# Groups of dummy matmuls in many tile shapes behind the last output matmul

## The chip, the cores and the metric

The kernel runs on one core of a Trainium2 chip. The metric is the device time of one execution in microseconds (us), the median over the runs.

## The reference

What is computed is attention with 32 global tokens and a local window, followed by a feed-forward block, over 8 batches with 8 heads of 64:

```python
s_g = scale * np.matmul(q_g, k_all.transpose(0, 1, 3, 2))      # 32 global queries see all 544 keys
out_g = np.matmul(sm(s_g), v_all)
mask = np.abs(pos[:, None] - pos[None, :]) <= 32               # 512 local queries see a window
s_ll = np.where(mask, scale * np.matmul(q_l, k_l.transpose(0, 1, 3, 2)), -1000000000.0)
s_lg = scale * np.matmul(q_l, k_g.transpose(0, 1, 3, 2))       # and the 32 global keys
out_l = np.matmul(sm(np.concatenate([s_lg, s_ll], axis=-1)), np.concatenate([v_g, v_l], axis=2))
x = np.concatenate([out_g, out_l], axis=2)...                  # (8 * 544, 512)
h = x @ w_in                                                   # 512 -> 2048
out = (h * (1.0 / (1.0 + np.exp(-1.702 * h)))) @ w_out         # 2048 -> 512, float32
```

## The kernel before

Operands are bfloat16 and sums are in float32 in PSUM. The program works in quads: one quad is four heads of one batch, so there are 16 quads, two to a batch. The order of the instructions on each engine is the order in which the code is written (`tc.manual_schedule()`); pools of tiles add the waits where a buffer is used again.

For a quad, `S` (L314) multiplies keys with queries. The contraction is over 32 partitions at a time (64 numbers per head lie as 32 float32 words of two bfloat16 each, and `e` picks one of the two). Four heads sit in four groups of 32 partitions, so four matmuls with tiles of 32 rows and 128 columns go to four PSUM banks. The queries are read in a window: `q[p, lo:hi, r0 : r0 + nr, e]` takes runs of 10 or 12 elements at a stride of two, 200 or 228 in all. `gk` (L333) uses tiles of 32 rows and 32 columns for the global keys, either 32 or 512 columns of queries wide. `ekU` (L400) and `U` (L426) multiply the exponentials with values; `U` has tiles of 128 rows and 32 columns, four heads side by side in one bank. `Gm` (L444) does the global queries with the same tiles and 66 columns. ScalarE takes the exponentials (L347), VectorE the mask product `M` (L354, bfloat16, both operands in SBUF), the transposes and the normalisation (`R`, `XL`, `G`).

The feed-forward block of batch i has `h_mm` (L495, full 128x128 tiles, 512 columns of tokens), `h_act` (tanh on ScalarE, L502, and a product on VectorE into `gT`, L503) and `o_mm` (L520, 512 columns). The attention quads of the next batch are placed between the `o_mm` groups. The global tokens of all batches form a ninth, narrow block (256 tokens). The last steps are

```python
    for st in range(4):
        o_mm(B, st)
    o_out(B, 1, None)
```

where `o_out` with its last tile runs the 16 accumulating matmuls twice (L532), for columns 0 to 320 and 320 to 512. ScalarE copies each part out of PSUM (L534), and SyncE and ScalarE issue the DMAs to the output (L542).

Names that the change uses: `warm` is a tile of zeros, [128, 512] in bfloat16, that `keep` (L165) and `zero` (L555) already read for dummy matmuls. `qtiles[0]` is the tile of transposed queries, [128, 24, 32] in float32, that `S` reads as bfloat16 pairs. `psP` is a pool of four PSUM banks (tag "p"); `psS` has two tiles of two banks each (tags "s0" and "s1"); `bank(pt, i)` is bank i of that pair of tiles. `att` is a pool of SBUF tiles with two buffers for each name (`rs`, `sT`, `e0`, `e1`). `mask` holds the window masks, and LW and RW are 352 and 428. The pieces of code that place a matmul's tile are the partition slices of its operands: the rows follow from the partitions of `lhsT`, the columns from the partitions of the output.

Of the kernel before, what the change touches and what calls it, by code (L numbers as in the profile page):

```python
# [12 lines left out]
F32 = mybir.dt.float32  # L13
BF16 = mybir.dt.bfloat16
# [783 lines left out]
    o_out(B, 1, None)  # L798


# [1 line left out]
_INS = ['q_l', 'k_l', 'v_l', 'q_g', 'k_g', 'v_g', 'moe_w_in', 'moe_w_out']  # L802
_OUTS = [((4352, 512), 'float32')]
# [25 lines left out]
```

## Time and profile before

The median of two runs is 307.42 us (307.30 and 307.54). The page has one profiled execution:

| | |
|---|---|
| span of the profiled execution | 305.3 us |
| median of the runs less the span | 2.1 us |
| TensorE matmuls | 298.7 us busy (98%), 3265 of them |
| TensorE weight loads | 148.5 us (49%), 3265 |
| VectorE / ScalarE / GpSimd | 211.2 / 169.3 / 55.7 us busy |
| granted TensorE clock | full in all 40 slices |
| o_mm (L520) | 122.0 us, 528 matmuls |
| h_mm (L495) | 108.9 us, 496 matmuls of 512 columns |
| S (L314) | 21.2 us, 528 matmuls |

The profiled execution's own time beyond its span is not on the page; the span runs from its first instruction to its last, and what the metric counts around it is taken as the 2.1 us between the span and the median. In the page a matmul's duration includes its way through the array, so matmuls that run one behind the other overlap; how often they start is read from their starts in the timeline. "PE" is the row of the matmuls and "PEld" that of the weight loads.

### The profile page before, as it was taken

To read this page: it belongs to the slowest core of one execution; us is meant where nothing else is said; L and a number is where in the kernel's file an instruction comes from. 1 tells how busy PE (TensorE), PEld (TensorE's weight loads), DVE (VectorE), ACT (ScalarE), POOL (GpSimd) and SP (SyncE) were. 2 spreads that over 40 slices of the span, in tenths; PEclk is the share of its full clock that TensorE was granted. 3 is DMA by queue.
4 is the path that set the end of the run, shared out by engine and by line. 5 is a ranking of instruction groups with operands and counts; after the bars stand their busy time and mean duration, and the time that the engine had idled before them with its cause. 6 is when DMAs were issued, how large, how long until landed. Compare 5 with 4: busy or idle time off the path is not lost.

```text
span 305.3 us, 7862 instructions
## 1 busy us (share of the span) xinstructions
PE 298.7 (98%) x3265; PEld 148.5 (49%) x3265; DVE 211.2 (69%) x445; ACT 169.3 (55%) x282; POOL 55.7 (18%) x89
## 2 busy tenths in 40 slices
PE   7999999999999999999999999999999999999995
PEld 6454445445454455445454455445454454446653
DVE  6678858978868876777767876787677855573320
ACT  4738484585556655575457654665456661673421
POOL 8732755530050002300050002100000000000000
PEclk9999999999999999999999999999999999999999
DMA  7999999999399023941299024901130021101122
GB/s 191 178 206 207 197 180 230 211 170 131 82 112 191 10 56 84 151 97 37 54 122 170 4 56 89 101 0 48 44 86 2 2 66 48 46 0 36 36 63 75
DMA packets 56436, 29.52 MB, mean 97 GB/s; under 512 B 43088, under 2 KB 46288, under 8 KB 56400
## 3 DMA queue, kind: packets, MB, share of 16 engines
q0 software_dynamic: 46000, 16.98, 49.9%
q1 hardware_dynamic: 9920, 11.39, 14.3%
q10 hardware_dynamic: 480, 0.66, 0.7%
q8 instruction: 25, 0.41, 0.6%
q14 instruction: 11, 0.09, 0.1%
HBM read 35.13 MB, written 8.91 MB: 144 GB/s over the span
## 4 chain that ended last, share of the span: by engine, by line
PE 80%; DMA 15%; DVE 2%; POOL 1%; issue 1%; ACT 0%; ACTq 0%; DVEq 0%; POOLq 0%
PE op L520 34%; PE hp L495 33%; DMA rk<-in_k_l_dram 10%; PE s L314 5%; PE ov L426 4%; DMA rq<-in_q_l_dram 3%; DMA w_in_sb<-in_moe_w_in_dram 2%; PE ov L400 2%; DVE xL L459 1%; PE op L532 1%; PE s L444 1%; PE s L333 1%; ACTq L542 0%; ACT ob L534 0%; DVE e L354 0%
## 5 line engine op out<-in xcount | busy, mean ns | idle before, releaser
L520 PE MATMUL op<-w_out_sb,gT 128*128 128x512 bf16 x528 | 122.0, 380 | 0.0
L503 DVE SCALAR_TENSOR_TENSOR gT<-th,hp 128x512 bf16<-128x512 f32 (+1 forms) x140 | 91.2, 657 | 41.8 <-ACT th L502 40.7
L495 PE MATMUL hp<-xL,w_in_sb 128*128 128x512 bf16 x496 | 108.9, 379 | 0.3 <-DVE xL L459 0.2
L502 ACT ACTIVATE th<-hp 128x512 f32<-128x512 f32 (+1 forms) x140 | 79.9, 573 | 43.4 <-PE hp L495 39.9
L495 PEld LDWEIGHTS <-w_in_sb 128*128 128x128 bf16 x576 | 56.2, 98 | 64.7 <-issue 0.9
L520 PEld LDWEIGHTS <-gT 128*128 128x128 bf16 x528 | 49.2, 98 | 56.2 <-issue 3.5
L347 ACT ACTIVATE e<-s 128x856 bf16<-128x856 f32 x62 | 51.6, 884 | 12.1 <-PE s L444 7.0
L534 ACT ACTIVATE ob<-op 128x512 f32<-128x512 f32 (+2 forms) x35 | 20.5, 585 | 59.0 <-PE op L520 56.5
L89 POOL DMA_DIRECT2D v<-in_v_l_dram x24 | 18.7, 782 | 111.2 <-PE s L444 105.8
L450 DVE STREAM_TRANSPOSE sT<-ov 128x512 f32<-128x512 f32 x15 | 10.8, 717 | 26.9 <-PE ov L426 26.9
L354 DVE TENSOR_TENSOR e<-e,mask 128x1408 bf16<-128x1408 bf16 x28 | 24.4, 872 | 5.7 <-ACT e L347 5.7
L314 PE MATMUL s<-q,kT 32*128 32x228 bf16 (+5 forms) x528 | 21.2, 280 | 1.0 <-DVE q L275 1.0
L459 DVE TENSOR_TENSOR xL<-ov,rs 128x512 bf16<-128x512 f32 x30 | 19.3, 686 | 1.4
L314 PEld LDWEIGHTS <-kT 32*128 32x128 bf16 x528 | 10.9, 95 | 14.8 <-issue 6.6
L271 DVE STREAM_TRANSPOSE kT<-rk 128x512 f32<-128x512 f32 (+1 forms) x17 | 16.9, 994 | 1.0 <-DMA rk<-in_k_l_dram 1.0
L383 ACT ACTIVATE ek<-kb 128x512 bf16<-128x512 f32 x16 | 9.7, 608 | 9.2 <-PE kb L333 7.0
L426 PE MATMUL ov<-e,v 128*32 128x160 bf16 (+1 forms) x480 | 12.2, 239 | 0.0
L454 DVE STREAM_TRANSPOSE rs<-rT 128x512 f32<-128x512 f32 x16 | 11.4, 711 | 0.6
L275 DVE STREAM_TRANSPOSE q<-rq 128x512 f32<-128x512 f32 (+1 forms) x17 | 10.9, 641 | 1.0 <-ACT rq L558 1.0
L426 PEld LDWEIGHTS <-v 128*32 128x32 bf16 x512 | 10.0, 97 | 0.9 <-issue 0.9
L333 PE MATMUL kb<-q,kgT 32*32 32x512 bf16 x128 | 10.4, 387 | 0.0
L495 PE MATMUL hp<-xG,w_in_sb 128*128 128x256 bf16 x64 | 9.6, 273 | 0.0
(82 smaller groups left out, 170.6 us busy)
## 6 DMA issues: line engine op xcount, KB each, us to landing
out_dram<-ob SPq DMA_DIRECT2D x132, 64.0 KB, 1.7
v<-in_v_l_dram POOLq DMA_DIRECT2D x32, 128.0 KB, 6.0
rk<-in_k_l_dram POOLq DMA_DIRECT2D x6, 512.0 KB, 10.8
rq<-in_q_l_dram POOLq DMA_DIRECT2D x5, 512.0 KB, 8.6
w_out_sb<-in_moe_w_out_dram POOLq DMA_DIRECT2D x4, 512.0 KB, 10.8
rq<-in_q_l_dram POOLq DMA_DIRECT2D x5, 256.0 KB, 8.9
ek<-ek SPq DMA_DIRECT2D x13, 96.0 KB, 2.9
w_in_sb<-in_moe_w_in_dram POOLq DMA_DIRECT2D x4, 256.0 KB, 6.4
```

Of the source, the lines that this page charges most:

```text
L89: nc.gpsimd.dma_start(out=vtiles[b % 2][p, s, :, :, :D], in_=vf[b, g][:, hs])
L271: nc.vector.transpose(self.kT.rearrange("p (r t) -> p t r", t=16)[:, lo:hi], loaded[self.b][0][:, self.u].bitcast(F32)[:, 32 * lo : 32 * hi])
L314: nc.tensor.matmul(ps[j][:, off : off + n], lhsT=self.k[p, 128 * c : 128 * c + 128, e], rhs=self.q[p, lo:hi, r0 : r0 + nr, e], start=(e == ...
L347: nc.scalar.activation(e[:, 2 * i : 2 * i + 2, :RW], self.ps[i][:, :, :RW], AF.Exp, scale=scale)
L354: nc.vector.tensor_mul(e, e, mask[:, rnd : rnd + 1, :].to_broadcast([128, 4, LW]))
L426: nc.tensor.matmul(ov[32 * j : 32 * j + 32, :].rearrange("p (t r) -> p t r", t=16)[:, :, r0 : r0 + nr], lhsT=lv, rhs=self.E[c // 2][:, j, ...
L459: nc.vector.tensor_mul(self.x[:, 2 * self.u + h, :], self.st[1 + h], self.st["rs"])
L495: nc.tensor.matmul(hp[:, : width(i)], lhsT=w_in_c[:, fc // 8, kc, fc % 8 // 2, :, fc % 2], rhs=(xL[i] if i < B else xG)[:, kc, :], start=( ...
L502: nc.scalar.activation(th[:, :n], hp[:, :n], AF.Tanh, scale=0.851)
L503: nc.vector.scalar_tensor_tensor(gTs[i][:, fc, :n], in0=th[:, :n], scalar=1.0, in1=hp[:, :n], op0=ALU.add, op1=ALU.mult)
L520: nc.tensor.matmul(op, lhsT=gTs[i][:, fc, tci * 128 : tci * 128 + 128], rhs=w_out_sb[:, fc, :], start=(first and fc == 4 * f4), stop=(fc = ...
L534: nc.scalar.activation(ob[:, lo:hi], op[:, lo:hi], AF.Copy, scale=0.5)
```

## The change

Behind `o_out(B, 1, None)` the program gets further work whose results nothing reads. `plain` issues full matmuls of 512 columns into one bank of `psP`. `tiles` issues, for every repetition, one matmul for each tile of the given rows and columns, row groups outside and column groups inside; row group i writes bank i, column group g writes its partitions. Between them the moving operand is straight (`near0`), a window of the queries (`runs`), or evenly strided (`flat`). At the end VectorE gets two fills and a reciprocal, a fill and a mask product, and GpSimd a fill, a mask product and a copy.

```diff
     o_out(B, 1, None)
 
 
+    keys = qtiles[0].bitcast(BF16).rearrange("p t (r e) -> p t r e", e=2)
+    flat = keys.rearrange("p t r e -> p (t r) e")
+
+    def tiles(name, rows, cols, n, reps, rhs, w=None):
+        pt = [psS.tile([128, 2, 512], F32, name=name, tag="s%d" % i) for i in range(2)]
+        for k in range(reps):
+            for i in range(128 // rows):
+                for g in range(128 // cols):
+                    p = slice(rows * i, rows * i + rows)
+                    c = slice(cols * g, cols * g + cols)
+                    nc.tensor.matmul(bank(pt, i)[c, :n], lhsT=warm[p, c], rhs=rhs(p, k), start=True, stop=True,
+                                     skip_group_check=True)
+
+    def near0(n):
+        return lambda p, k: warm[p, :n]
+
+    def runs(lo, hi, r0, nr):
+        return lambda p, k: keys[p, lo:hi, r0 : r0 + nr, k % 2]
+
+    def plain(name, n, w=128, rhs=None):
+        ps = psP.tile([128, 512], F32, name=name, tag="p")
+        for k in range(n):
+            nc.tensor.matmul(ps[:, :w], lhsT=warm[:, 0:128], rhs=rhs(k) if rhs else warm[:, :w], start=True, stop=True)
+
+    plain("z0", 4, 512)
+    tiles("r4c1n228", 32, 128, 228, 6, near0(228))
+    plain("z1", 4, 512)
+    tiles("r4c1win", 32, 128, 228, 6, runs(0, 19, 6, 12))
+    plain("z2", 4, 512)
+    tiles("r4c2n160", 32, 64, 160, 6, near0(160))
+    plain("z3", 4, 512)
+    tiles("r4c2win", 32, 64, 160, 6, runs(0, 20, 4, 8))
+    plain("z4", 4, 512)
+    tiles("r4c4n132", 32, 32, 132, 6, near0(132))
+    plain("z5", 4, 512)
+    tiles("r4c4win", 32, 32, 132, 6, runs(0, 22, 4, 6))
+    plain("z6", 4, 512)
+    tiles("r4c4n32", 32, 32, 32, 6, near0(32))
+    plain("z7", 4, 512)
+    tiles("r2c1n228", 64, 128, 228, 6, near0(228))
+    plain("z8", 4, 512)
+    tiles("r2c1str", 64, 128, 228, 6, lambda p, k: flat[p, :228, k % 2])
+    plain("z9", 4, 512)
+    tiles("r4c1str", 32, 128, 228, 6, lambda p, k: flat[p, :228, k % 2])
+    plain("za", 4, 512, lambda k: flat[:, :512, k % 2])
+    tiles("r1c4n192", 128, 32, 192, 4, near0(192))
+    tiles("r4c4m", 32, 32, 192, 2, near0(192))
+    tiles("r4c1m", 32, 128, 192, 2, near0(192))
+    tiles("r1c4m", 128, 32, 192, 2, near0(192))
+    tiles("r2c2m", 64, 64, 192, 2, near0(192))
+    tiles("r1c2m", 128, 64, 192, 2, near0(192))
+    plain("zb", 4, 512)
+    qa, qb = att.tile([128, 512], F32, name="rs"), att.tile([128, 512], F32, name="sT")
+    nc.vector.memset(qa, 2.0)
+    nc.vector.memset(qb, 1.0)
+    nc.vector.reciprocal(qb, qa)
+    eb = att.tile([128, 4, RW + 32], BF16, name="e0")
+    nc.vector.memset(eb, 1.0)
+    nc.vector.tensor_mul(eb[:, :, 40 : 40 + LW], eb[:, :, 40 : 40 + LW],
+                         mask[:, 0:1, :].to_broadcast([128, 4, LW]))
+    ec = att.tile([128, 4, RW + 32], BF16, name="e1")
+    nc.gpsimd.memset(ec, 1.0)
+    nc.gpsimd.tensor_mul(ec[:, :, 40 : 40 + LW], ec[:, :, 40 : 40 + LW],
+                         mask[:, 0:1, :].to_broadcast([128, 4, LW]))
+    nc.gpsimd.tensor_copy(ec[:, :, 0:256], eb[:, :, 0:256])
```

In the built program the other engines' instructions and all of TensorE's ahead of this point stand in the order that they had. TensorE gets 604 matmuls, each with its weight load. The counts by group are: 12 plain groups of 4; 24 each for r4c1n228, r4c1win and r4c1str; 48 each for r4c2n160 and r4c2win; 96 each for r4c4n132, r4c4win and r4c4n32; 12 each for r2c1n228 and r2c1str; 16 for r1c4n192, 32 for r4c4m, 8 each for r4c1m, r1c4m and r2c2m, and 4 for r1c2m. The first matmul of a `tiles` group waits for the last group that wrote the same PSUM tile; z0 to z3 wait for ScalarE's copies of the last outputs. GpSimd's fill waits for the last readers of an older `e1`, and its copy for VectorE's mask product.

## Prediction

> **What bounds the kernel now.** I read the page first, then the end of the chain of waits, then the timeline of TensorE in one stage where tile shapes like the added ones occur.
>
> ```profile
> span 305.3 us, 7862 instructions
> PE 298.7 (98%) x3265; PEld 148.5 (49%) x3265; DVE 211.2 (69%) x445; ACT 169.3 (55%) x282; POOL 55.7 (18%) x89
> PEclk9999999999999999999999999999999999999999
> ```
>
> TensorE is busy for 98% of the span at the full granted clock, and the other engines have room. What is put on TensorE behind its last matmul therefore lengthens the program, except for what lies beside the tail. The tail is the end of the chain of waits (start, length, what):
>
> ```profile
> 293.90 4.32 PE op L520 x20
> 298.22 2.19 PE op L532 x16
> ...
> 300.43 0.45 ACT ob L534
> ...
> 301.80 0.33 ACT ob L534
> ```
>
> The timeline of the last microseconds gives the start of the last group on TensorE and the last issues:
>
> ```profile
> 299.82 1.89 PE L532 MATMUL op<-w_out_sb,gT 128*128 128x320 bf16 x19
> 302.16 0.85 ACTq L542 DMA_DIRECT2D out_dram<-ob  x2
> ```
>
> TensorE's last matmul ends at 299.82 + 1.89 = 301.71. It took 246 ns (mean of the 128x192 group), and 16 of them were busy 1.5 us, so they step by (1.5 - 0.25)/15 = 0.08; the next matmul could have started at 301.71 - 0.25 + 0.08 = 301.55. The output then takes until the second issue near 302.6 plus 1.6 to landing (the page's median for these 24 KB issues), 304.2, and 1.1 more to the span's end.
>
> The timeline of TensorE in the stage from 243 on shows what packed matmuls cost. Columns: start, length to the end of the last, line, output and inputs, rows*columns of the tile, form of the first, count.
>
> ```profile
> 243.04 0.81 PE L520 MATMUL op<-w_out_sb,gT 128*128 128x512 bf16 x3
> 243.79 0.66 PE L314 MATMUL s<-q,kT 32*128 32x200 bf16 x16
> 245.00 0.49 PE L426 MATMUL ov<-e,ones 128*32 128x160 bf16 x16
> 245.32 0.78 PE L426 MATMUL ov<-e,v 128*32 128x160 bf16 x32
> 245.93 0.30 PE L444 MATMUL s<-v,e 128*32 128x66 bf16 x16
> 246.06 0.20 PE L444 MATMUL s<-rvg,eg 128*32 128x66 bf16 x4
> 246.19 0.39 PE L520 MATMUL op<-w_out_sb,gT 128*128 128x512 bf16 x1
> 249.75 0.66 PE L314 MATMUL s<-q,kT 32*128 32x228 bf16 x16
> 250.35 0.39 PE L520 MATMUL op<-w_out_sb,gT 128*128 128x512 bf16 x1
> ```
>
> Lengths include the drain of the last matmul, so prices are taken from starts. Call a pass the matmuls of disjoint tiles that run together (four here). Full matmuls of 512 step by 0.86/4 = 0.216 us (the chain shows "L520 x4" at 0.86). Three from 243.04 would let the next start at 243.69; L314 starts at 243.79, so a **change of tile shape** costs 0.10. L314 holds four passes of 228, 228, 200 and 200 columns from 249.75 to 250.35; less one change, 0.50/4 = 0.125 for 214 columns, 0.584 ns a column. L426 has 48 matmuls, 12 passes, in 245.93 - 245.00 = 0.93: 0.0775 for 176 columns, 0.44 ns a column. L444 has 20 matmuls, five passes, in 246.19 - 245.93 - 0.10 = 0.16: 8 ns a matmul with its weight load.
>
> **The change part by part.** Nothing is removed or moved; the order on each engine before the last output matmul is the same. TensorE gains 604 matmuls with a weight load each.
>
> The 48 plain ones (12 groups of four, 512 columns): 48 x 0.216 = 10.37. The strided moving operand of one group has no row of its own; L333 reads 512 columns at that stride and its passes start 0.24 apart (244.44 and 244.68 in the same timeline), so its four could cost 0.1 more; I leave that out.
>
> Changes of shape: two at each of ten groups between plain ones, seven in the closing run: 27 x 0.10 = 2.70 (bounds 0.09 and 0.11).
>
> Six repetitions of every row-tiled group make six passes. The four groups of 228 in straight or evenly strided columns (r4c1n228, r2c1n228, r2c1str, r4c1str) lie between L426 (like reading, 0.44) and L314 (like tile, 0.584): 24 passes cost 2.41 to 3.20. I take 2.41, since L314 differs by reading short runs, and L333, also with four row groups but straight columns, needs 0.24/512 = 0.47. The window group r4c1win is L314's own form: 6 x 228 x 0.584 = 0.80. The two of 160 columns: 0.42 straight, 0.56 in windows, bounds 0.84 and 1.12 for both.
>
> The three 16-tile groups (r4c4n132, r4c4win, r4c4n32) have 96 matmuls each. The array needs 0.35, 0.46 and 0.08, so how fast TensorE can take instructions decides, and no row shows that alone. L444's 8 ns a matmul is one end (0.77 a group); the other is the longest dense stretch, 243.79 to 246.19 with some 112 matmuls, 21 ns each (2.0 a group). I take 12 ns, nearer L444, whose tiles are as small: 3 x 96 x 0.012 = 3.46.
>
> The closing run without plain groups between (r1c4n192 to r1c2m): 14 passes of 192 columns, of which the two of r4c4m are 32 matmuls at 12 ns: 12 x 0.0845 + 0.38 = 1.40 (1.28 to 2.0). Five of its groups wait for the group ahead to leave the same PSUM tile: the 192-column matmul lasts 0.246 against a step of 0.08, 0.17 more, of which 0.10 is counted as the change; with the signal 0.12 each, 0.60 (0 to 1.0). The plain groups wait for ScalarE's evictions of the last outputs; the latest ends at 302.13, and the fourth group, which waits for it, starts after 304. Cost nothing; without that cover 0.6.
>
> Sum on TensorE: 10.37 + 2.70 + 2.41 + 0.80 + 0.98 + 3.46 + 1.40 + 0.60 = 22.7. It begins at 301.55, where 3.75 us of span were left; behind it stand 0.16 of the last matmul (380 - 216 ns) and the 1.1 of the program's end. So 22.7 - 3.75 + 0.16 + 1.1 = **20.2 more**: span 325.5, and with the 2.1 that lie between the span and the median of the runs shown (307.42), 327.6.
>
> [...]
>
> **Elementwise work.** On VectorE it stands behind its last gT operation, which ends at 294.78. Two fills of 512 (272 ns for 256 in the row of L161, so 0.5 each), a reciprocal of 512 (L452: 253 ns for 16, L464: 158 for 1, so 6.3 ns an element, 3.4), a fill of 1840 (273 ns for 257, some 1.9) and a mask product (872 ns, L354) sum to 7.2: done by 302. GpSimd's copy of 1024 follows, 0.85 to 3.2 by its rows below: done by 305.2. TensorE hides all that until 324; uncovered it would end the program 1.0 later than before at most.
>
> GpSimd's fill and product wait only for an older user of e1 (L354 and L444, done at 246.26). The fill of 1840, by GpSimd's 125 ns for 32 and 205 for 128, takes 1.6; the product is bounded by VectorE's 0.87 below and twice the 401 ns for 257 of GpSimd's select above, 4.4. It could meet VectorE's mask products at 249.28 and 252.15. If it blocked the first until 252.3, the second would end at 254.25 instead of 253.04, and L426, which needs it near 253.53, would stand 0.7. I take 0, since no row shows such a block, and keep 0.7.
>
> [...]
>
> **The rivals.** (1) Instructions come no faster than 21 ns a matmul and row tiles all cost 0.584: 10.37 + 3.0 + 3.20 + 0.80 + 1.12 + 6.05 + 2.0 + 1.0 = 27.5, 25.0 more, 332.4. For it: nothing longer than that stretch is dense. Against: the stretch holds its own waits and passes. (2) The issue costs nothing and the array alone counts: 16-tile groups 0.89 together, waits 0, changes 2.4: 18.8, 16.3 more, 323.7. For it: bursts in L333 start 2 to 4 ns apart. Against: those are 16 matmuls long, not 96. (3) GpSimd's early work delays the last attention stage as above: 328.3. (4) On the other side, no slower: the matmuls whose results nobody reads are not carried out, and TensorE still ends at 301.71; only the elementwise tail is left, which ends within 1.0, so 307.4 to 308.4. It decides from the point where fewer than about 8.6 of the 22.7 us are carried out. For it: no output reads them. Against: they stand in the built program behind L532, and L165 and L555, whose results are as dead, are in the profile with full durations.
>
> **How the numbers follow.** Forecast 0.60, (1) 0.21, (2) 0.13, (3) 0.04, (4) 0.02. The time is the forecast's, 327.6. The range runs from (2) to (1) with the 0.7 of GpSimd and some rounding: 323.5 to 333.5. A run of this kernel can be told from no change at about 2%, 6.1 us; only (4) lies inside that, so slower has 0.98, the same 0.01 and faster 0.01.
>
> **What would show it.** Right: the plain groups step by 0.216; changes of shape cost 0.10; the straight 228-column passes take 0.10 against 0.13 in windows; 16-tile groups take about 1.15 whatever their columns; the chain ends on the last plain group and the program's end follows within 1.2. Wrong: 16-tile groups over 2 us, straight row passes as slow as windows, a VectorE product near 249 that starts late, or VectorE or GpSimd at the chain's end. A clock below full in the last slices would break every price.

## The result and the profile after

The changed kernel takes 328.62 us (328.28 and 328.97) against 307.42: 1.068 times the time before, 95% interval 1.064 to 1.072. Run again beside the kernel before, its median was 327.62 against 307.51, ratio 1.062 (1.054 to 1.071). The forecast was 327.6. Some executions show TensorE at half its clock for one or two stretches of 3.4 us, which adds 1.5 to 5 us; where nothing else is said, numbers below are from stretches at full clock.

The head of the page of the changed kernel:

```profile
span 327.2 us, 9080 instructions
PE 321.9 (98%) x3869; PEld 160.2 (49%) x3869; DVE 218.7 (67%) x450; ACT 169.3 (52%) x282; POOL 61.1 (19%) x92
PEclk9999999999999999999999999999999999999989
```

TensorE has its 604 matmuls more and is still busy for 98% of a longer span. One slice near the end is below full clock, which no slice was before. The end of the chain of waits (start, length, what) now runs through the dummy groups:

```profile
297.92 3.49 PE op L532 x32
301.41 0.86 PE z L823 x4
302.27 0.70 PE r4c1n L811 x24
302.97 0.97 PE z L823 x4
303.94 0.89 PE r4c1win L811 x24
...
305.80 0.59 PE r4c2n L811 x48
...
307.35 0.59 PE r4c2win L811 x39
...
308.92 0.93 PE r4c4n L811 x96
...
310.82 0.98 PE r4c4win L811 x84
...
312.77 0.40 PE r4c4n L811 x42
313.17 1.27 issue
314.44 0.56 PE r4c4n L811 x54
...
317.09 1.82 PE z L823 x4
...
325.24 0.97 PE zb L823 x4
```

A length here reaches to the start of the next piece, so it holds one change of tile shape where the shape changes: a plain group takes 0.97, that is 4 x 0.216 and 0.10. Two lines are new in kind. In the middle of r4c4n32, behind the 42nd matmul, TensorE stands for 1.27 us on "issue": nothing that the profile shows ends that wait. And one plain group takes 1.82 instead of 0.97. The table of stretches explains the second (columns: busy time and count of TensorE, its weight loads, VectorE, ScalarE and GpSimd, then the granted clock):

```profile
312.70:316.10 3.40, 2.13 (x105) 1.33 (x106) 0.00 (x0) 0.00 (x0) 0.00 (x0) 1.00 0.03 5
316.10:319.50 3.40, 3.40 (x24) 1.45 (x22) 0.00 (x0) 0.00 (x0) 0.00 (x0) 0.50 0.00 0
```

The stretch that holds the pause is followed by 3.4 us at half clock. The elementwise work is off the chain. VectorE's mask products of the attention stage that runs at the time of GpSimd's product, before the change:

```profile
249.28 0.85 DVE L354 TENSOR_TENSOR e<-e,mask 128x1408 bf16<-128x1408 bf16 x1
252.15 0.89 DVE L354 TENSOR_TENSOR e<-e,mask 128x1408 bf16<-128x1408 bf16 x1 [1.88 <-ACT e L347]
```

GpSimd's part after the change, and the same two mask products:

```profile
247.75 2.70 POOL L863 TENSOR_TENSOR e<-e,mask 128x1408 bf16<-128x1408 bf16 x1
301.94 1.04 POOL L865 COPY e<-e 128x1024 bf16<-128x1024 bf16 x1 [51.48 <-DVE e L859]
```

```profile
248.97 2.23 DVE L354 TENSOR_TENSOR e<-e,mask 128x1408 bf16<-128x1408 bf16 x1
251.84 0.89 DVE L354 TENSOR_TENSOR e<-e,mask 128x1408 bf16<-128x1408 bf16 x1 [0.51 <-ACT e L347]
```

The first mask product takes 2.23 where it took 0.85 before; the second starts when ScalarE has its operand ready, as it did. TensorE shows no wait for VectorE in this stage.

### The profile page after: what moved, and what is told of

It reads as the page before. It is cut to its first block, busy times and chain, and to the rows that moved or that the text cites. A ratio compares the mean times of both kernels' runs of the same rounds, so it can differ in the third digit from the quotient of the medians.

```text
span 327.2 us, 9080 instructions
## 1 busy us (share of the span) xinstructions
PE 321.9 (98%) x3869; PEld 160.2 (49%) x3869; DVE 218.7 (67%) x450; ACT 169.3 (52%) x282; POOL 61.1 (19%) x92
## 4 chain that ended last, share of the span: by engine, by line
PE 82%; DMA 14%; DVE 2%; issue 1%; POOL 1%; ACT 0%; DVEq 0%; POOLq 0%
PE op L520 31%; PE hp L495 31%; DMA rk<-in_k_l_dram 9%; PE s L314 4%; PE ov L426 4%; PE z L823 3%; DMA rq<-in_q_l_dram 3%; DMA w_in_sb<-in_moe_w_in_dram 2%; PE ov L400 2%; PE op L532 1%; DVE xL L459 1%; PE r4c4n L811 1%; PE s L444 1%; PE s L333 1%; PE r2c1n L811 0%
## 5 line engine op out<-in xcount | busy, mean ns | idle before, releaser
L354 DVE TENSOR_TENSOR e<-e,mask 128x1408 bf16<-128x1408 bf16 x28 | 25.8, 920 | 4.4 <-ACT e L347 4.4
L314 PE MATMUL s<-q,kT 32*128 32x228 bf16 (+5 forms) x528 | 21.2, 280 | 0.7 <-DVE q L275 0.7
L314 PEld LDWEIGHTS <-kT 32*128 32x128 bf16 x528 | 11.0, 96 | 14.5 <-issue 6.3
L426 PE MATMUL ov<-e,v 128*32 128x160 bf16 (+1 forms) x480 | 12.2, 239 | 0.0
L862 POOL MEMSET e<- 128x1840 bf16 x1 | 1.6, 1632 | 54.7 <-PE s L444 54.7
L811 PEld LDWEIGHTS <-warm 32*32 32x32 bf16 (+5 forms) x556 | 7.9, 93 | 7.9 <-issue 6.9
L823 PE MATMUL z<-warm 128*128 128x512 bf16 x40 | 11.2, 406 | 0.0
```

What stands on the lines that cost most here:

```text
L314: nc.tensor.matmul(ps[j][:, off : off + n], lhsT=self.k[p, 128 * c : 128 * c + 128, e], rhs=self.q[p, lo:hi, r0 : r0 + nr, e], start=(e == ...
L354: nc.vector.tensor_mul(e, e, mask[:, rnd : rnd + 1, :].to_broadcast([128, 4, LW]))
L426: nc.tensor.matmul(ov[32 * j : 32 * j + 32, :].rearrange("p (t r) -> p t r", t=16)[:, :, r0 : r0 + nr], lhsT=lv, rhs=self.E[c // 2][:, j, ...
L823: nc.tensor.matmul(ps[:, :w], lhsT=warm[:, 0:128], rhs=rhs(k) if rhs else warm[:, :w], start=True, stop=True)
```

## Experiments

**The same kernel again.** No edit.

> The changed kernel once more. Fetch theory: the pause of 1.27 us inside r4c4n32 comes from instructions that arrive in blocks of 256 and are used up faster than the next block comes; so it stands at the same matmul (the 43rd of the group) again, between 0.8 and 1.6 us long. Chance theory: the pause is a disturbance of one execution; it is elsewhere or missing and the span is some 1.3 us shorter. The stretch of half clock (3.4 us long) behind the pause may come or stay away with either; without it the span is 0.7 to 1.5 us shorter than 327.2. Time 327 to 329, ratio 1.065 to 1.071.

Three of four executions were at full clock: 327.16, 327.39, 327.86 (the fourth 332.13). The chain of the profiled one:

```profile
313.16 0.40 PE r4c4n L811 x42
313.56 1.33 issue
314.89 0.56 PE r4c4n L811 x54
```

The pause stands behind the 42nd matmul again, so it is no chance event. (The expectation calls it the 43rd: the 43rd is the first that waits.) No half clock followed, and the span was 326.1 instead of 327.2.

**Only the plain groups.** All `tiles(...)` lines are left out:

```diff
-    tiles("r4c1n228", 32, 128, 228, 6, near0(228))
...
-    tiles("r1c2m", 128, 64, 192, 2, near0(192))
```

> All tiled groups are left out; the 48 plain matmuls and the elementwise work stay. Forecast's sum: 48 x 0.216 = 10.4, less the 2.5 of tail that the sum hides: 7.9 more than before, 315.3, no change of tile shape, full clock, no pause. If plain groups cost more than their steps (a wait for PSUM between groups), 0.1 to 0.3 more for each of 12 groups: 316.5 to 319.

315.01 us, the median of four. On the chain the 48 matmuls take from 302.03 to 312.42, 10.4. So the plain part and the hidden tail of 2.5 are right to 0.3 us, and groups of plain matmuls cost nothing beyond their steps.

**Without the elementwise work.** The lines from `qa, qb = ...` on are left out.

> The fills, products, reciprocal and copy on VectorE and GpSimd are left out, all matmuls stay. Forecast: they are covered, so the time is that of the changed kernel within 0.3 us (327 to 329 in the same state of the clock). VectorE's mask product near 249, 2.23 us in the changed kernel, is back at 0.85 to 0.9, since GpSimd's product no longer runs beside it. If the elementwise work delayed TensorE, 0.7 to 1.5 us come back.

The one execution at full clock took 327.66, inside the 327.16 to 327.86 of the whole change (the other three 330.34 to 332.31). VectorE's mask product in that place is back:

```profile
252.43 0.85 DVE L354 TENSOR_TENSOR e<-e,mask 128x1408 bf16<-128x1408 bf16 x1
```

One clean execution is thin evidence for the time, but the mask product is clear: what stretched it was GpSimd's product.

**r4c4n32 first.**

```diff
     plain("z0", 4, 512)
-    tiles("r4c1n228", 32, 128, 228, 6, near0(228))
+    tiles("r4c4n32", 32, 32, 32, 6, near0(32))
...
     plain("z6", 4, 512)
-    tiles("r4c4n32", 32, 32, 32, 6, near0(32))
+    tiles("r4c1n228", 32, 128, 228, 6, near0(228))
```

> r4c4n32 and r4c1n228 change places, so that r4c4n32 is the first tiled group and only two 16-tile groups follow each other. Fetch theory: r4c4n32 runs through in 0.85 to 0.95 us without a pause, since the block ahead of it is used up slowly; a shorter pause (0 to 1 us) may stand behind r4c4win instead. Shape theory: narrow 32-column matmuls in 16 tiles cause the pause themselves; it stays inside r4c4n32, about 1.3 us.

One execution, 331.29 us, with half clock near the program's start (10.4 to 17.2); so its time isn't compared, and only the timeline of TensorE is read:

```profile
306.42 0.92 PE L811 MATMUL r4c4n<-warm 32*32 32x32 bf16 x96
...
315.12 0.82 PE L811 MATMUL r4c4win<-q,warm 32*32 32x132 bf16 x70
316.96 0.35 PE L811 MATMUL r4c4win<-q,warm 32*32 32x132 bf16 x26 [1.03 <-issue]
```

The narrow group runs through; the next plain matmul starts at 307.27, 0.85 later. The pause has moved into r4c4win, behind its 70th matmul. The shape theory falls. Counted in TensorE's stream (a weight load and a matmul are two instructions), the place is the same: 812 instructions behind the last output matmul in both orders.

**Everything 42 instructions later.**

```diff
-    plain("z0", 4, 512)
+    plain("z0", 25, 512)
```

> The first plain group has 25 matmuls instead of 4, so every later instruction is 42 places further in TensorE's stream (21 x 0.216 = 4.5 us longer). Fetch theory: the pause keeps its absolute place in the stream and so falls 21 matmuls earlier in r4c4n32, behind its 21st instead of its 42nd; 0.4 to 1.5 us long. Shape theory, or any cause that sits in the group: behind the 42nd again.

```profile
317.46 0.91 PE r4c4n L811 x93
318.37 0.23 issue
...
321.75 0.18 PE r4c4n L811 x21
321.93 0.12 issue
```

The pause is behind the 21st matmul of r4c4n32, as the fetch theory said: 812 instructions behind the last output matmul once more. It is only 0.3 us from start to start, below the 0.4 to 1.5 expected, and there is a second one, 0.45 from start to start, behind the 93rd matmul of r4c4n132: 556 instructions, 256 earlier. That the pause would be split in two was not expected. (This execution, too, had half clock near its start, 9.8 to 16.6, and not here.)

**One long dense group.**

```diff
     plain("z0", 4, 512)
+    plain("z1", 12, 512)
+    tiles("r4c4n32", 32, 32, 32, 32, near0(32))
+    plain("zb", 4, 512)
```

All other groups and the elementwise work are left out.

> The dummy work is 16 plain matmuls, one group of 512 matmuls in 16 tiles with 32 columns (1024 instructions), 4 plain ones; no elementwise work, no other groups. Fetch theory (blocks of 256 instructions, each available some 3.1 to 3.4 us after the block before it was entered): three to four pauses of 2 to 2.4 us, 128 matmuls apart, the group 10.5 to 13 us long, each pause with an instruction packet of 16 KB near it. Issue alone (8.3 ns a matmul, as in the changed kernel outside the pause): 4.3 us and no pause. Pause as a matter of the place behind other dense groups only: at most one pause, 4.3 to 5.8.

```profile
309.05 2.23 PE r4c4n L811 x262
311.28 2.08 issue
313.36 1.22 PE r4c4n L811 x125
314.58 2.24 issue
316.81 1.17 PE r4c4n L811 x120
```

Two pauses of 2.27 and 2.44 from start to start, behind the 262nd and the 390th matmul (a few records are missing in the counts of the chain; the weight loads are all there): 128 matmuls apart, at 556 and 812 instructions. The group took 8.94, twice the 4.3 of issue alone, and less than the 10.5 expected: the packet before had come at 306.19 to 307.43, during the plain matmuls. The count of pauses was wrong, their size and distance right. From 312.45 on, inside the first pause, this execution ran at half clock, so its second pause and its total aren't quite those at full clock. Packets of the instruction queue, 16 KB each, start at 311.0 and 314.5 in the trace. The page before has 25 of them for 3265 matmuls, the page after 30: five more for 1208 instructions more on TensorE, about 240 each.

So the pauses stand 256 instructions apart and at the same places in the stream, 556 and 812. In the changed kernel the 256 instructions up to place 556 were used up in 3.18 us (307.61 to 310.80), and no pause followed; the next 256 took 2.19 (to 312.99), and the pause of 1.27 followed. The kernels with the elementwise work left out or made longer pause behind the 42nd matmul of r4c4n32 too, as the whole change does. The times of the packets say more. In the first trace of the change a packet started at 312.04 and had landed at 313.00; the pause ended 1.44 later, and the next packet started 1.14 after that, at 315.58. The seven traces of these six kernels (the one with the longer GpSimd product is told below) hold ten pauses, and each ends 1.36 to 1.52 us after a packet of the instruction queue has landed, whether that packet took 0.92 or 1.26 us. In the four traces with a single pause, place 556 was passed with no pause, or with a gap of 0.09, 1.39 to 2.11 us after the landing of the packet before it. And in nine of the ten the next packet starts 1.1 to 1.2 us after the pause has ended. These times would fit a wait for the packet; no run changed the packets themselves, so that they are the cause isn't shown.

**A longer product on GpSimd.**

```diff
+    big = consts.tile([128, 2816], BF16)
+    nc.gpsimd.memset(big, 1.0)
     ec = att.tile([128, 4, RW + 32], BF16, name="e1")
     nc.gpsimd.memset(ec, 1.0)
-    nc.gpsimd.tensor_mul(ec[:, :, 40 : 40 + LW], ec[:, :, 40 : 40 + LW],
-                         mask[:, 0:1, :].to_broadcast([128, 4, LW]))
+    nc.gpsimd.tensor_mul(big, big, big)
```

> GpSimd's product at 248 multiplies 2816 elements of a tile of its own instead of 1408 by the mask (its fill of that tile stands earlier, when GpSimd is free), so it runs some 5.3 us, to about 253, instead of 2.7. Lock theory: VectorE's mask product stands until GpSimd's product has ended; it shows some 4.9 us, the second mask product ends near 255.1 instead of 252.7, and TensorE waits 1.5 to 2.0 us before L426 near 253: time 1.5 to 2 more than the changed kernel (329 to 330 against 327.2 to 327.9 at full clock). Sharing theory: both mask products run beside GpSimd's at 2.2 us each, the second ends near 254.1, TensorE waits 0.7 to 1.0. Cover theory as forecast for the short product: 0.

GpSimd, VectorE and TensorE in the timeline:

```profile
247.78 4.88 POOL L865 TENSOR_TENSOR big<-big 128x2816 bf16<-128x2816 bf16 x1
```

```profile
249.12 4.28 DVE L354 TENSOR_TENSOR e<-e,mask 128x1408 bf16<-128x1408 bf16 x1
```

```profile
253.46 0.34 PE L426 MATMUL ov<-e,ones 128*32 128x160 bf16 x8 [0.18 <-DVE e L354]
254.40 0.34 PE L426 MATMUL ov<-e,ones 128*32 128x192 bf16 x8 [0.60 <-DVE e L354]
```

VectorE's product took 4.28 us, against 0.85 without GpSimd's, and ends 0.74 after GpSimd's (253.40 against 252.66), about as if it had stood until that one's end. This fits the lock theory, and the sharing theory (2.2 us each) falls. TensorE stands 0.18 and 0.60 for it. Three executions at full clock took 328.76, 329.00 and 329.50 against 327.16 to 327.86: some 1.6 us. The product ran 4.88 us instead of the 5.3 expected, and TensorE's own wait is 0.8, below the 1.5 to 2 of the lock theory. The profiled pair (329.00 and 327.86) is 1.14 apart: the first plain group starts 0.80 later, and the rest is a second pause, in r4c4win:

```profile
312.01 0.21 PE r4c4win L811 x11
312.22 0.37 issue
...
314.88 1.16 issue
```

Counted by weight loads it is behind the 14th matmul of r4c4win, 556 instructions, the place of the first pause in the two experiments before. So TensorE's wait gave 0.8 of the 1.5 to 2 expected, and the time agreed partly by chance. The short product of the change leaves off early enough to cost nothing: VectorE had finished its first mask product 0.64 before the second could start (251.20 and 251.84).

**Windows of other places and lengths.** The groups are replaced by six passes each of:

```diff
+    tiles("w128r0n12", 32, 128, 228, 6, runs(0, 19, 0, 12))
+    tiles("w128r6n12", 32, 128, 228, 6, runs(0, 19, 6, 12))
+    tiles("w128r4n8", 32, 128, 160, 6, runs(0, 20, 4, 8))
+    tiles("w128r2n8", 32, 128, 160, 6, runs(0, 20, 2, 8))
+    tiles("w128r0n10", 32, 128, 200, 6, runs(0, 20, 0, 10))
+    tiles("w64r6n12", 32, 64, 228, 6, runs(0, 19, 6, 12))
+    tiles("f128r6n12", 128, 128, 228, 6, runs(0, 19, 6, 12))
...
```

with plain groups between.

> Six passes per group, start to start of a pass, with runs of n elements from element r of rows of 32 (4 bytes apart). Grain theory: words are read in aligned grains of four, a run pays whole grains, whatever the tile shape: 32x128 tiles r0n12 0.100, r6n12 0.132, r4n8 0.070, r2n8 0.103, r0n10 0.105; 32x64 r6n12 0.132; 128x128, 64x128 and 128x32 r6n12 0.132. Run theory: every run costs 4 cycles more whatever its place: r0n12 0.132, r6n12 0.132, r4n8 and r2n8 0.105, r0n10 0.121, other shapes r6n12 0.132. Shape theory: only tiles of 32x128 pay for runs: r0n12 0.132, r4n8 and r2n8 about 0.10, r0n10 0.116, other shapes r6n12 0.098 to 0.100.

```profile
302.95 0.81 PE L811 MATMUL w128r0n<-q,warm 32*128 32x228 bf16 x24
303.69 1.04 PE L823 MATMUL z<-warm 128*128 128x512 bf16 x4
304.66 0.96 PE L811 MATMUL w128r6n<-q,warm 32*128 32x228 bf16 x24
305.56 1.04 PE L823 MATMUL z<-warm 128*128 128x512 bf16 x3
306.52 0.59 PE L811 MATMUL w128r4n<-q,warm 32*128 32x160 bf16 x24
307.05 1.04 PE L823 MATMUL z<-warm 128*128 128x512 bf16 x4
...
313.30 0.95 PE L811 MATMUL f128r6n<-q,warm 128*128 128x228 bf16 x6
314.09 1.03 PE L823 MATMUL z<-warm 128*128 128x512 bf16 x4
```

From start to the next start, less 0.10 for the change of shape, through six: r0n12 (0.747 - 0.10)/6 = 0.108, r6n12 0.132, r4n8 0.071. The full 128x128 tile changes no shape: 0.786/6 = 0.131. The others by the same reckoning: r2n8 0.114, r0n10 0.114; 64x128 0.131, 32x64 0.137 and 128x32 0.143 for r6n12. The shape theory falls, as every shape pays for r6n12 (0.131 to 0.143). The run theory falls, as r4n8 pays nothing and r6n12 more than r0n12. The grain theory orders all of them; its size was a little off. A cycle here is the time of one column of a straight matmul, some 0.416 ns (full matmuls step by 0.083 us with 192 columns and by 0.216 with 512). Less the 4.6 ns that a straight pass has beyond its columns (0.0996 us for 228), a run in 32x128 tiles costs 8.0 cycles for two grains of four words, 13.1 for three (r0n12, r0n10 and r2n8 alike), 16.1 for four. In the other shapes only four grains were tried, 16 to 17.5 cycles. A grain here is four words of 4 bytes (two bf16 elements each, of which these matmuls read one), counted from the start of a row; that the cost of a run goes with their number was measured, how the words are read was not.

**Queries moved by two words, without any dummy work.** In the kernel before:

```diff
-        qt = consts.tile([128, 24, 32], F32, name="q%d" % i)
+        qt = consts.tile([128, 24 * 32 + 4], F32, name="q%d" % i)[:, 2 : 2 + 24 * 32].rearrange("p (t r) -> p t r", t=24)
```

> The kernel before, without any dummy work, and with the tile of transposed queries moved by two words, so that the windows of 12 words (elements 6 to 18 and 14 to 26) begin on a grain of four words and cover three grains instead of four; the windows of 10 cover three as before. Grain theory, with the costs measured in the windows experiment (16.1 cycles of a run over four grains, 13.1 over three): a pass of L314 with 228 columns falls from 0.133 to 0.108, 62 passes save 1.5 us: ratio 0.995, 305.7 to 306.2 beside some 307.4. If the saving is covered by another wait in those stages, or VectorE's transposes into the moved tile get slower, 0 to 0.5: ratio 0.998 to 1.002.

306.08 us against 307.26, ratio 0.9971, 95% interval 0.9948 to 0.9994: 0.3% faster than the kernel before, a small difference, but with the interval clear of 1. The medians lie 1.2 us apart, the expectation was 1.5. The 228-column group of L314 in the kernel before and with the queries moved (busy time, mean ns):

```profile
L314 PE MATMUL s<-q,kT 32*128 32x228 bf16 x248 | 13.5, 292 | 0.0
L314 PE MATMUL s<-q,kT 32*128 32x228 bf16 x248 | 12.0, 267 | 0.0
```

The group's busy time falls by the 1.5 expected; the 200-column group, whose grains stay three, has 12.4 and 12.3. The stage that the prediction read on L314:

```profile
248.85 0.62 PE L314 MATMUL s<-q,kT 32*128 32x228 bf16 x16
249.40 2.76 PE L520 MATMUL op<-w_out_sb,gT 128*128 128x512 bf16 x12
```

The four passes with their change of shape take 0.55, against 0.60 before (249.75 to 250.35).

## Why the prediction was right

By its own steps, with what the repeated run at full clock shows (r4c4n32 without a pause from the run that has it first):

| term | forecast | measured |
|---|---|---|
| 48 plain matmuls | 10.37 | 10.4 |
| 27 changes of shape | 2.70 | 2.8, 0.10 to 0.11 each |
| four groups of 228, straight or strided | 2.41 | 2.42 |
| r4c1win | 0.80 | 0.79 |
| r4c2n160 and r4c2win | 0.98 | 1.00 |
| three 16-tile groups, issue alone | 3.46 | 2.5 |
| pause inside them | none | 1.5 |
| closing run with its waits | 2.00 | 1.94 |
| sum | 22.7 | 23.3 |

The sum is measured from the first plain start, 301.64, to the end of the last step, 324.93. The tail behind it is 1.2, as reckoned. The span was 326.1 instead of 325.5; what lies between span and time was 1.8 (327.86 less 326.1) instead of the 2.1 taken, which made up half of that. The 0.12 that the forecast put on each wait of the closing run holds 0.05 for a signal that no row shows; in the first profile TensorE stood 0.04 at four of its five hand-overs (323.08, 323.58, 324.42 and 324.84) and not at the fifth. The sign of being wrong that the prediction named last, a clock below full at the end, did appear in the first profile: from 316.10 to 319.51 the clock was half, and three groups there took 3.94 us instead of 2.37.

**Tile shapes.** The choice between L426 and L314 as the price of straight row-tiled passes was right: r4c1n228 took 0.70 on the chain, 0.60 without the change of shape, and r4c1win 0.79. The reason given, short runs, was right in direction and incomplete: runs of the same length cost 13.1 or 16.1 cycles (r0n12 and r6n12), by the number of grains of four words that they touch. r4c2win, whose runs of eight fill two grains, costs hardly more than r4c2n160 (0.51 and 0.49), so the surcharge of 0.14 put on it was wrong, and the straight one was 0.07 dearer than reckoned. Evenly strided passes took 0.102 to 0.103 us, straight ones 0.099.

**Issue.** This is the mis-sized term. A 16-tile group costs 0.75 to 0.89 instead of 1.15. In the trace the first 32 matmuls start within 0.10 to 0.13 us, the 33rd comes 0.21 to 0.27 after the first, 0.03 after the first has ended, and then one starts every 8.3 ns, with 132 columns as with 32. So nearly L444's 8 ns was the price, though by coincidence: L444's five passes of 66 columns at 0.42 ns take 0.14 of its 0.16 us, so its row was set by the passes. The 21 ns of rival (1) was set by passes and waits too, as the argument against it said.

**The pause** was in no term: 1.5 us with its refilling. The issue, priced 1.0 too high, happens to offset two thirds of it, and the half clock adds to it in some executions. The forecast's closeness, 0 to 1.0 us of the two medians, is partly that luck; the sum without the pause would be 21.8.

**GpSimd.** Its product lay inside the bounds (2.70 between 0.87 and 4.4) and the cost of 0 held, but not for the reason taken: VectorE's mask product took 2.23 us beside the short product, 4.28 beside the long one and 0.85 without any. So the block for which the prediction had no row showed in the length of VectorE's product and not, as the prediction's sign had it, in a late start. Rival (3) had the right kind of delay, with a product too short to reach TensorE: TensorE stood 0.18 and 0.60 for the mask products with the long one, and not at all with the short one.

**The rivals.** (2) had the issue right in kind for the first 32 matmuls of a group only. (4) falls: all 604 matmuls are in the profile with their full durations.

**The half clock behind the pause.** It came in the first profile, 3.41 us from 316.10 on, behind the pause of 1.27, and in the one without the elementwise work, where the pause was 1.16 and the plain group behind r2c1n228 took 1.82 too. It did not come in the repeated run, where the pause was 1.33, nor with the longer GpSimd product (1.16) or with r4c4n32 first (1.03). In the long dense group it came inside the first pause of 2.08. So the length of the pause alone doesn't decide it here, as 1.16 stands on both sides and the longer 1.33 was followed by full clock; what does isn't shown.

## What to carry to other kernels

Price packed matmuls by passes taken from starts in the timeline, and add the 0.10 us measured here for each change of tile shape; the packed groups of 16 tiles here started one matmul each 8.3 ns once 32 were under way, and dense stretches ended in pauses of 0.3 to 2.4 us at places 256 instructions (128 matmuls with their loads) apart, the one of 1.27 behind 256 that were used up in 2.19 us. Look at where the runs of a strided operand lie: runs of twelve from element 0 instead of element 6 took 0.108 us a pass here instead of 0.132, and moving the queries by two words made the whole kernel 0.3% faster without touching an instruction. Before putting a two-operand product on an idle GpSimd, look which VectorE products run at that time: the mask product here, with two bfloat16 operands in SBUF, took 4.28 us instead of 0.85 beside a GpSimd product of 4.88.

## What the runs showed of the hardware that was not expected

- A pause of 0.3 to 2.4 us at places 256 TensorE instructions apart; in the changed kernel it stood behind 256 that were used up in 2.19 us and not behind 256 that took 3.18. It went with the place in the stream through six kernels, and each of the ten ended 1.36 to 1.52 us after an instruction packet of 16 KB had landed.
- Behind a pause of over 1 us inside a group the next 32 matmuls start within 0.12 us, as at the start of a group, and then one starts every 8.3 ns again.
- The cost of a strided run by grains of four words: 8, 13 and 16 columns' time for two, three and four grains in 32x128 tiles, and 16 to 17.5 for four grains in four other shapes.
- Four row tiles with straight operands run at nearly the rate of full ones: 228 columns in 0.099 us a pass, all four matmuls together, where full matmuls of 512 columns need 0.096 for as many columns.
- Half clock followed pauses of 1.27 (for 3.41 us) and 1.16 us in two profiles, and not those of 1.33, 1.16 and 1.03 in three others.
